# Softmax rows turned by VectorE in 32x32 blocks of 32-bit pairs instead of by TensorE, dense rows laid as 128 half rows, the maximum subtracted also on GpSimd

## The chip, the cores and the metric

One core of a Trainium2 chip. The metric is device microseconds (us) of one execution. The kernel before takes 1591.72 us (median of 3 runs, 1589.29 to 1592.78).

## The reference, cut to what matters

The input x has 2048 rows of 512 numbers. Two equal layers follow each other; each adds a recurrent attention and then a dense layer:

```python
x = x + A(layernorm(x)); x = x + B(layernorm(x))     # twice, with the same weights

def A(x):                        # 64 segments of 32 rows, in order
    mem = mem0                   # 8 rows
    for s in range(64):
        h = concat([mem, x[32*s : 32*s + 32]])        # L = 40 rows
        q, k, v = h @ Wq, h @ Wk, h @ Wv              # 32 heads of 128
        scores = where(mask, q @ k.T / sqrt(128), -1e9)     # 40 x 40 per head
        o = softmax(scores) @ v                       # per head
        o = o @ Wo                                    # summed over the heads, 40 x 512
        mem = o[:8]; out[s] = o[8:]
def B(x): return relu(x @ w1) @ w2                    # 512 -> 1376 -> 512
```

The memory of segment s is needed by segment s + 1, so the segments of one layer can't run side by side.

## The kernel before, in words

**Steps.** The kernel runs 66 steps. In step k it handles segment k of the first layer and segment k - 2 of the second (`DELTA = 2`), in the code the two values of `a`; in the first and last two steps only one is there. `HT` holds the 2 x 40 columns of both, transposed, so most matmuls have 80 columns.

**One step.** `queries_keys` makes q and k of eight or four heads at a time (TensorE, L726, from `HT`), evicted to `qT` and `kT` (`copy_op`, on ScalarE L982 or VectorE L984). The heads go in five units (`UNITS`): three of 8 heads and two of 4. For each unit `scores` does the softmax: score matmuls into PSUM (L1133), mask added (`block`, L1144), row maximum (`top`, L1148), subtraction (`sub`, L1151), exponential on ScalarE (`exp`, L1155), row sum (`total`, L1158), reciprocal (`recip`, L1161), scaling into `P` (`mul`, L1175, on VectorE or GpSimd). P has the queries of a head on the partitions, two heads of a pair at partitions 0 and 64. `turn` (L1181) multiplies each 128-column piece of P with an identity on TensorE, which turns it; `keep` copies the result twice from PSUM to `PT` (ScalarE L1198 or VectorE L1200), each time with one half of the partitions set to zero by `half`. `attend` multiplies the values (`V0` and `vw`) with PT (L1217), its result is evicted to `OT`, and `project` sums all heads into one PSUM bank (`st`). From that bank 16 columns go back into the next step's `HT` (the memories) and 64 into `OX`.

**The dense layer** of the step (`finish`) comes later, beside the next step's attention: `OX` is turned by a DMA into `y` (64 rows of 512), added to `x` (L924), normalized (`layernorm`: L749, L752, on GpSimd L731 and L736, then L755), turned by TensorE, multiplied with `w1` and `w2`; `total` (L940) adds the result in two halves of 256 columns, the second read from partition 64 of PSUM. The first layer's rows are normalized again and become columns of `HT` two steps later; the second layer's rows are narrowed on GpSimd and stored by one DMA.

**The order** is fixed before the kernel runs. `Plan.order` goes through all operations with an estimated cost for each (`t_dve(n)`, 0.07 us and 1.042 ns an element; `t_act`, `t_pool`) and writes them out; every engine then executes its own list strictly in that order and waits on semaphores. The tables `PLACE` (order of the TensorE operations by step and phase; phase 0 is a middle step), `PAIRED` (which matmuls run as two halves of 64 columns of weights) and `AHEAD` (priorities) steer it. An operation with two engines, such as `sub` after the change, gets its engine in that plan.

The score-side PSUM pool `b_work` has five banks; `scores` takes one for the scores (`sp`) and one for the turned rows (`tp`).

Of the kernel before, what the change touches and what calls it, by code (L numbers as in the profile page):

```python
# [9 lines left out]
F32 = mybir.dt.float32  # L10
# [20 lines left out]
LOOK = 0.0763052  # L31
PERIOD = 26.155362
PLACE = {
# [185 lines left out]


def t_dve(n, rate=1):
    return 0.07 + 1.042e-3 * n / rate


PART, MASKED = {ACT: 0.13, DVE: 0.10}, {ACT: 0.11, DVE: 0.065}
XBAR = 0.5, 0.2, 2.6


def t_pool(n):
    return 0.06 + 2.2e-3 * n  # L230

# [213 lines left out]
def kernel(  # L445
# [193 lines left out]
    def prepare():  # L639

        def zero_none():
            nc.vector.memset(none[:], 0.0)
# [733 lines left out]
```

## Time and profile before

| | us |
|---|---|
| median of 3 runs (lowest, highest) | 1591.72 (1589.29, 1592.78) |
| span of the profiled execution, first to last instruction | 1588.6 |
| TensorE matmul (PE), busy | 1569.5 |
| TensorE weight load (PEld), busy | 1411.1 |
| ScalarE (ACT), busy | 1165.2 |
| VectorE (DVE), busy | 1082.3 |
| GpSimd (POOL), busy | 314.3 |

The page gives the span as the only time of the profiled execution; it is 3.1 us under the median of the runs. A busy time is the union of an engine's instructions. Matmuls are pipelined: an 80-column matmul is recorded with some 200 ns, but 128 of them in a row take 4.61 us in the chain, 36 ns each. So a matmul's price is its distance to the next one, not its recorded duration, and the same holds in part for VectorE, where one instruction can start before the one ahead of it has ended.

### The profile page before, as it was taken

To read this page: it belongs to the slowest core of one execution; us is meant where nothing else is said; L and a number is where in the kernel's file an instruction comes from. 1 tells how busy PE (TensorE), PEld (TensorE's weight loads), DVE (VectorE), ACT (ScalarE), POOL (GpSimd) and SP (SyncE) were. 2 spreads that over 40 slices of the span, in tenths; PEclk is the share of its full clock that TensorE was granted. 3 is DMA by queue.
4 is the path that set the end of the run, shared out by engine and by line. 5 is a ranking of instruction groups with operands and counts; after the bars stand their busy time and mean duration, and the time that the engine had idled before them with its cause. 6 is when DMAs were issued, how large, how long until landed. Compare 5 with 4: busy or idle time off the path is not lost.

```text
span 1588.6 us, 100346 instructions
## 1 busy us (share of the span) xinstructions
PE 1569.5 (99%) x45458; PEld 1411.1 (89%) x45458; DVE 1082.3 (68%) x2957; ACT 1165.2 (73%) x3073; POOL 314.3 (20%) x667
## 2 busy tenths in 40 slices
PE   8999999999999999999999999999999999999998
PEld 5689999999999989999989999999998998898887
DVE  4566766766776776686676677677667667667665
ACT  4667777777777777777777777777777777777774
POOL 5112112212112212121121221211211121112110
PEclk9999999999999999999999999999999999999999
DMA  9711111111111111111111111111111111111100
GB/s 371 243 44 30 26 33 32 29 35 37 25 39 31 35 29 33 29 32 40 26 36 27 35 26 42 37 26 38 25 35 28 33 33 29 33 25 22 28 21 9
DMA packets 76540, 70.89 MB, mean 45 GB/s; under 512 B 50920, under 2 KB 62416, under 8 KB 76112
## 3 DMA queue, kind: packets, MB, share of 16 engines
q1 hardware_dynamic: 70096, 44.14, 13.1%
q0 software_dynamic: 4992, 19.40, 3.4%
q8 instruction: 356, 5.83, 1.6%
q10 hardware_dynamic: 1024, 0.93, 0.2%
q14 instruction: 72, 0.59, 0.1%
HBM read 31.53 MB, written 9.96 MB: 26 GB/s over the span
## 4 chain that ended last, share of the span: by engine, by line
PE 97%; DMA 1%; DVE 1%; POOL 1%; ACT 0%; issue 0%; DVEq 0%; POOLq 0%
PE work L726 40%; PE st L726 19%; PE fill L1048 16%; PE fill L726 8%; PE fill L821 5%; PE work L1217 5%; PE work L1133 4%; DMA xg<-in_A_x_dram 0%; DMA y<-OX 0%; DMA w_sb<-in_B_w_dram 0%; ACT HT L982 0%; POOL Wo_sb L537 0%; PE fill L711 0%; DVE ln L749 0%; POOL ln L736 0%
## 5 line engine op out<-in xcount | busy, mean ns | idle before, releaser
L726 PE MATMUL work<-HT,Wq_sb 128*128 128x80 bf16 (+2 forms) x10400 | 361.8, 201 | 3.1 <-ACT HT L982 3.1
L726 PE MATMUL work<-HT,Wk_sb 128*128 128x80 bf16 (+2 forms) x10416 | 362.7, 201 | 0.8 <-ACT HT L982 0.8
L726 PEld LDWEIGHTS <-Wq_sb 128*128 128x128 bf16 (+1 forms) x10400 | 330.9, 104 | 20.8 <-issue 6.0
L726 PE MATMUL st<-OT,Wo_sb 128*128 128x80 bf16 (+1 forms) x8448 | 345.5, 201 | 0.0
L726 PEld LDWEIGHTS <-Wk_sb 128*128 128x128 bf16 (+1 forms) x10416 | 327.1, 104 | 17.3 <-issue 2.0
L726 PEld LDWEIGHTS <-Wo_sb 128*128 128x128 bf16 x8448 | 315.7, 100 | 13.0 <-issue 12.7
L1048 PE MATMUL fill<-Wv_sb,HT 128*64 128x512 bf16 x2112 | 273.6, 381 | 1.1 <-DVE HT L984 1.0
L982 ACT CAST kT<-work 128x320 bf16<-128x320 f32 (+1 forms) x523 | 218.3, 418 | 68.6 <-PE work L726 31.1
L982 ACT CAST qT<-work 128x320 bf16<-128x320 f32 (+1 forms) x516 | 215.7, 418 | 67.5 <-PE work L726 47.2
L1198 ACT ACTIVATE PT<-work,half 128x160 bf16<-128x160 f32 (+1 forms) x515 | 231.3, 463 | 20.1 <-PE work L726 12.7
L982 ACT CAST OT<-work 128x320 bf16<-128x320 f32 (+1 forms) x461 | 186.2, 420 | 50.7 <-PE work L1217 50.6
L982 ACT CAST vw<-fill 128x512 bf16<-128x512 f32 x229 | 134.1, 586 | 113.3 <-PE fill L1048 109.8
L1144 DVE TENSOR_TENSOR es<-work,maskb 128x320 f32<-128x320 f32 (+2 forms) x330 | 136.2, 413 | 99.7 <-PE work L1133 93.2
L924 DVE TENSOR_TENSOR xg<-xg,y 64x512 f32<-64x512 f32 x65 | 44.2, 680 | 227.2 <-DMA y<-OX 226.6
L731 POOL TENSOR_SCALAR ln<-ln 32x1 f32<-32x1 f32 (+2 forms) x159 | 46.6, 293 | 566.7 <-DVE ln L752 561.0
L1155 ACT ACTIVATE es<-es 128x320 f32<-128x320 f32 (+2 forms) x330 | 136.1, 413 | 24.4 <-DVE es L1151 16.2
L1048 PEld LDWEIGHTS <-HT 128*64 128x64 bf16 x2112 | 98.9, 110 | 57.0 <-DVE HT L984 1.2
L1151 DVE TENSOR_TENSOR es<-es,mx 128x320 f32<-128x320 f32 (+2 forms) x330 | 136.3, 413 | 4.9
L1148 DVE TENSOR_REDUCE mx<-es 128x8 f32<-128x320 f32 (+2 forms) x330 | 133.9, 406 | 5.4
L1158 DVE TENSOR_REDUCE sm<-es 128x8 f32<-128x320 f32 (+2 forms) x330 | 133.4, 404 | 5.1 <-ACT es L1155 2.2
L1175 DVE TENSOR_TENSOR P<-es,sm 128x320 bf16<-128x320 f32 (+1 forms) x269 | 126.9, 472 | 3.3
L1133 PEld LDWEIGHTS <-qT 128*40 128x40 bf16 x4096 | 93.3, 97 | 35.6 <-ACT qT L982 13.6
(96 smaller groups left out, 2164.8 us busy)
## 6 DMA issues: line engine op xcount, KB each, us to landing
V<-vw SPq DMA_DIRECT2D x248, 48.0 KB
V<-vh SPq DMA_DIRECT2D x120, 64.0 KB
Wq_sb<-in_A_Wq_dram POOLq DMA_DIRECT2D x2, 2048.0 KB, 23.2
Wk_sb<-in_A_Wk_dram POOLq DMA_DIRECT2D x2, 2048.0 KB, 28.6
Wo_sb<-in_A_Wo_dram POOLq DMA_DIRECT2D x2, 2048.0 KB, 39.4
vh<-vg SPq DMA_DIRECT2D x32, 128.0 KB
xb<-in_A_x_dram SPq DMA_DIRECT2D x16, 128.0 KB
Wv_sb<-in_A_Wv_dram POOLq DMA_DIRECT2D x1, 2048.0 KB, 13.2
```

What stands on the lines that cost most here:

```text
L726: nc.tensor.matmul(out_[u:v, :], lhsT=lhsT[:, u:v], rhs=rhs, start=start, stop=stop, tile_position=(0, u), **more)
L821: nc.tensor.matmul(yp[64 * u:64 * u + 64, 0:256], lhsT=hT[:, fc, :], rhs=w2_sb[:, fc, 256 * u:256 * u + 256], start=(fc == 0), stop=(fc == ...
L982: nc.scalar.copy(out=out_, in_=in_)
L1048: nc.tensor.matmul(vp[64 * b:64 * b + 64, :], lhsT=cols(c4), rhs=Wv_sb[:, c4, n * 512:(n + 1) * 512], start=(c4 == 0), stop=(c4 == NC4 - 1 ...
L1133: nc.tensor.matmul(v[64 * g2:64 * g2 + L, a, i, b, :], lhsT=qT[:, hi, a * L:(a + 1) * L], rhs=kT[:, hi, a * L:(a + 1) * L], start=True, st ...
L1144: nc.vector.tensor_tensor(out=flat(es[:, A]), in0=flat(sp[:, A]), op=ALU.add, in1=maskb[:, a_lo:a_hi, :].unsqueeze(2).to_broadcast([128, n ...
L1148: nc.vector.tensor_reduce(out=mx[:, As], in_=es3(), axis=AX.X, op=ALU.max)
L1151: nc.vector.tensor_tensor(out=es3(), in0=es3(), op=ALU.subtract, in1=mx[:, As].unsqueeze(2).to_broadcast([128, ns * na, L]))
L1155: nc.scalar.activation(out=es[:, A], in_=es[:, A], func=ACTF.Exp, scale=SCALE)
L1158: nc.vector.tensor_reduce(out=sm[:, As], in_=es3(), axis=AX.X, op=ALU.add)
L1175: (nc.gpsimd if eng == POOL else nc.vector).tensor_tensor(out=o, in0=flat(es[:, A]), op=ALU.mult, in1=sm[:, As].rearrange("p (a s) -> p a ...
L1198: nc.scalar.activation(out=o, in_=i, func=ACTF.Copy, scale=half[:, b:b + 1])
```

## The change

- `turn` leaves TensorE. The two heads of a pair now lie next to each other as 16-bit numbers (index g, innermost), so that a pair of them is one 32-bit word, and VectorE's `transpose`, which turns each 32x32 block of 32-bit words by itself, turns two heads at once. Six instructions a unit: two over 64 partitions (64 words a row and pair of heads), which put all blocks, and four over 32 partitions, which write the blocks off the diagonal to their right place. Their inputs and outputs start at partitions 0, 32, 64 or 96. `PT` is zeroed once at the start, the masking copies (`keep`) and the bank `tp` are gone, and `attend` reads PT with a step of two elements.
- For that order the score tile is read from PSUM, the maximum and the sum from SBUF, with g innermost or with a step of two. `mul` of a unit of 8 heads becomes two instructions.
- `sub` may go to GpSimd or VectorE.
- The rows of the dense side are laid as 128 half rows (64 partitions for each 256 of the 512 columns, every other 128): `add`, the statistics, the normalization and `total` handle 256 elements on 128 partitions; the partial statistics are exchanged between the halves (`swap`, two small copies on ScalarE or VectorE). The turning matmuls are two instead of four. GpSimd's copies and the store are split into two.
- Memory is shared out anew (`y` and `ob` lie in `vx`, `none` in `P3`), and `PLACE`, `PAIRED`, `AHEAD` and `LOOK` are new numbers.

The core of the diff (the tables, the memory layout and the start are left out):

```diff
@@ layernorm of half rows, new
+    def layernorm_halves(x, keys, quick=False):
...
+            nc.vector.bn_stats(out=ln[:, 0:6], in_=x[:, :])
+        def swap(eng):
+            for u in range(2):
+                copy_on(eng, ln[64 * u:64 * u + 64, 8:14], ln[64 - 64 * u:128 - 64 * u, 0:6])
+        def aggr():
+            nc.vector.bn_aggr(out=ln[:, 6:8], in_=ln[:, :].rearrange("p (s f) -> p s f", s=2)[:, :, 0:6])
+        def norm():
+            nc.vector.tensor_scalar(out=xn[:, 0:256], in0=x[:, :], scalar1=ln[:, 6:7], scalar2=ln[:, 7:8],
+                                    op0=ALU.subtract, op1=ALU.mult)
@@ finish
         def add():
-            nc.vector.tensor_tensor(out=x[RB, :], in0=x[RB, :], in1=y[RB, :], op=ALU.add)
+            nc.vector.tensor_tensor(out=x[:, :], in0=x[:, :], in1=y[:, 0:256], op=ALU.add)
         def total(to):
-            for u in range(2):
-                cs = slice(256 * u, 256 * u + 256)
-                nc.vector.tensor_tensor(out=to[RB, cs], in0=x[RB, cs], in1=yp[64 * u:64 * u + 64, 0:256], op=ALU.add)
+            nc.vector.tensor_tensor(out=to[:, :], in0=x[:, :], in1=yp[:, 0:256], op=ALU.add)
@@ scores
         def block():
-            nc.vector.tensor_tensor(out=flat(es[:, A]), in0=flat(sp[:, A]), op=ALU.add,
-                                    in1=maskb[:, a_lo:a_hi, :].unsqueeze(2).to_broadcast([128, na, ns, L]))
+            nc.vector.tensor_tensor(out=ekg(), in0=sp[:, A].rearrange("p (j g k) -> p j k g", k=L, g=2), op=ALU.add,
+                                    in1=maskb[:, mine, :].unsqueeze(3).to_broadcast([128, nx * na, L, 2]))
...
-        plan.op(DVE, t_dve(n), sub, r=[mx], w=[es])
+        plan.op((POOL, DVE), (t_pool(n), t_dve(n)), sub, r=[mx], w=[es])
...
+        pieces = [(a, a + 1) for a in range(a_lo, a_hi)] if nx == 2 else [(a_lo, a_hi)]
         def mul(eng):
...
-        def turn(cols):
-            rhs = ident[:, :].rearrange("p (g q) -> p g q", g=2)[:, :, 0:L]
-            for a in range(a_lo, a_hi):
-                for i, x in enumerate(xs):
-                    z = nx * a + i
-                    c0 = 256 * a + 128 * x
-                    across(cols, tp[:, z * 2 * L:(z + 1) * 2 * L], P[:, c0:c0 + 128], rhs)
-        for b in range(2):
-            def keep(eng, b=b):
...
+        def turn():
+            i = P[:, 0:512].bitcast(F32).rearrange("p (j k) -> p j k", k=64)[:, mine, :]
+            o = PT[:, 0:nx * na, :, :].bitcast(F32)
+            for b in range(2):
+                R = slice(64 * b, 64 * b + 64)
+                nc.vector.transpose(out=o[R, :, b, :], in_=i[R, :, :])
+            for b in range(2):
+                R0, R1 = slice(64 * b, 64 * b + 32), slice(64 * b + 32, 64 * b + 64)
+                nc.vector.transpose(out=o[R0, :, b, 32:64], in_=i[R1, :, 0:32])
+                nc.vector.transpose(out=o[R1, :, b, 0:32], in_=i[R0, :, 32:64])
+        plan.op(DVE, 2 * t_dve(64 * na * nx) + 4 * t_dve(32 * na * nx), turn,
+                r=[*[("P", p, b, x) for b in range(2) for x in xs], "PT0"], w=[PT])
@@ attend
-                                             rhs=PT[:, a, 2 * i + h2, :, :], start=True, stop=True, tile_position=(0, u))
+                                             rhs=PT[:, (a - a_lo) * nx + i, :, :].rearrange("p b (q g) -> p b q g", g=2)[:, :, 0:L, h2],
+                                             start=True, stop=True, tile_position=(0, u))
@@ some of the new PLACE for a middle step, in their order
...
+    ("queries_keys.mmu1.2", 0): 65.109
...
+    ("scores.mmu1.0", 0): 66.065
+    ("scores.mmu0.0", 0): 67.104
+    ("scores.mmu2.0", 0): 67.827
+    ("scores.mmu3.0", 0): 72.231
+    ("scores.mmu4.0", 0): 77.413
+    ("attend.mmu1.0", 0): 81.682
+    ("attend.mmu0.0", 0): 81.683
+    ("attend.mmu2.0", 0): 84.931
+    ("attend.mmu3.0", 0): 87.378
+    ("attend.mmu4.0", 0): 87.783
+    ("project.mm.4", 0): 90.115
...
```

More of the change, by code (lines that the diff above doesn't have):

```diff
@@ new lines @@
+    ("*layernorm.aggr", 1): -21903.3, ("*make_mask", 1): -103617.438, ("*prepare_more.zero_ox", 1): 1.534,
+    ("*rstd.power", 1): 15.001, ("*rstd.raise_", 1): -61376.175, ("*turned.keep", 1): -24955.153,
+    ("*turned.turn", 1): 118381.72, ("*values.ev", 1): 0.807, ("*zero_columns.zero", 1): 0.064,
+    ("attend.ev", 0): -0.293, ("attend.ev", 1): 0.579, ("attend.ev", 2): -0.123, ("attend.mm", 1): 0.399,
+    ("attend.mm", 2): 1.152, ("bulk.land", 1): 26.171, ("clear_x.clear", 1): 20655.056,
@@ new lines @@
+    ("dense_layer.mm.da", 0): 0.236, ("dense_layer.mm.da", 2): 48.945, ("dense_layer.relu.da", 0): 100982.711,
+    ("dense_layer.relu.da", 1): 0.845, ("dense_layer.relu.da", 2): -11.721, ("finish.add", 1): -96751.759,
+    ("finish.narrow.db", 0): -0.422, ("finish.store.da", 2): -0.297, ("finish.store.db", 0): -10.15,
+    ("finish.total_out.da", 2): -52594.789, ("finish.total_x.da", 0): 2.7, ("finish.turn", 0): -40.658,
+    ("finish.turn", 1): -2.025, ("finish.turn", 2): 9.243, ("finish.turn_near", 2): -2.902,
@@ new lines @@
+    ("finish.widen", 0): -1.484, ("finish.widen", 1): 45455.413, ("get_x", 1): -82953.917, ("idle.spins", 2): -0.588,
+    ("late_values.mm", 0): 1.257, ("late_values.put", 0): 23.681, ("layernorm.aggr", 0): -28.708,
+    ("layernorm.aggr.dl", 0): 56094.205, ("layernorm.aggr.dl", 1): 83.393, ("layernorm.norm.dl", 1): 0.066,
+    ("layernorm.stats", 0): -254390.254, ("layernorm.stats.dl", 0): 2.212, ("layernorm.stats.dl", 1): 1.455,
+    ("layernorm_halves.aggr.da", 0): -7022.782, ("layernorm_halves.aggr.da", 2): -47028.151,
@@ new lines @@
+    ("prepare.place", 1): 9.977, ("prepare.turn", 1): 67303.233, ("prepare.zero", 1): 0.326,
+    ("prepare.zero_none", 1): 0.229, ("prepare_late.load", 0): -7.502, ("project.ev", 1): -6.419,
+    ("project.ev", 2): 64646.14, ("project.first", 1): -16.097, ("project.mm", 1): 2.102, ("project.mm", 2): 0.027,
+    ("project.rows", 0): -2.141, ("project.rows", 2): 0.044, ("queries_keys.ev", 0): 13.389,
+    ("queries_keys.ev", 1): -33.964, ("queries_keys.ev", 2): 0.003, ("queries_keys.mm", 0): -59260.586,
@@ new lines @@
+    ("scores.mul", 0): -0.605, ("scores.mul", 1): 47.888, ("scores.mul", 2): 58322.939,
+    ("scores.recip", 0): 96086.484, ("scores.recip", 1): -6.261, ("scores.recip", 2): 41.387,
+    ("scores.sub", 0): -142237.316, ("scores.sub", 1): -33204.156, ("scores.sub", 2): 1.026,
+    ("scores.top", 0): 154356.569, ("scores.top", 1): 8.385, ("scores.top", 2): 0.507,
+    ("scores.total", 0): -61524.001, ("scores.total", 1): 19.349, ("scores.total", 2): -4.942,
+    ("scores.turn", 1): 50960.199, ("scores.turn", 2): 19.857, ("turned.keep", 0): 0.081,
@@ L199 @@
+    ("turned.keep.da", 0): -14.11, ("turned.keep.da", 2): 53.845, ("turned.keep.db", 0): -0.106,
+    ("turned.keep.db", 1): -0.015, ("turned.turn", 0): -48305.91, ("turned.turn.da", 0): -2472.454,
+    ("turned.turn.da", 1): -6.507, ("turned.turn.da", 2): -71771.416, ("turned.turn.db", 0): -231.019,
+    ("turned.turn.db", 1): -6.756, ("values.ev", 0): -1.484, ("values.ev", 2): -20.456, ("values.mm", 0): 0.229,
+    ("values.mm", 1): -2.61,
 }
@@ L222, in t_dve @@
     return 0.07 + 1.042e-3 * n / rate
-PART, MASKED = {ACT: 0.13, DVE: 0.10}, {ACT: 0.11, DVE: 0.065}
+PART = {ACT: 0.13, DVE: 0.10}
 XBAR = 0.5, 0.2, 2.6
@@ L641, in zero_none @@
         def zero_none():
-            nc.vector.memset(none[:], 0.0)
+            nc.vector.memset(none[:, :], 0.0)
         def make_half():
@@ L671, in prepare @@
         plan.available("memory", 5.5)
-        plan.op(DVE, 0.17, zero_none, w=["none", "set"])
+        plan.op(DVE, 0.30, zero_none, w=["none", "set", *[("P", 3, b, x) for b in range(2) for x in range(2)]])
         plan.op(DVE, 0.4, make_half, w=["half", "set"])
@@ L676, in prepare @@
         parts = [([V0], 0.92, [("V0", q, b) for q in range(4) for b in range(2)] + [("V0l", b) for b in range(2)])]
-        parts += [([t], 0.30, [("P", p, b, x) for b in range(2) for x in range(2)]) for p, t in enumerate(Pt)]
+        parts += [([t], 0.30, [("P", p, b, x) for b in range(2) for x in range(2)]) for p, t in enumerate(Pt[:3])]
+        parts += [([t], 0.6, ["PT0"]) for t in p_PT.tiles]
         for tiles, t, w in parts:
@@ L710, in spin @@
         for u in range(2):
-            nc.tensor.matmul(bank[:, 256 * u:256 * u + 256], lhsT=none[:, 0:128], rhs=none[:, :], start=True, stop=True)
+            nc.tensor.matmul(bank[:, 256 * u:256 * u + 256], lhsT=none[:, 0:128], rhs=none[:, 0:256], start=True, stop=True)
     def idle(t, r=()):
@@ L762, in layernorm, with stats, turned @@
         return xn
-    def turned(xn, n, columns, copies):
+    def layernorm_halves(x, keys, quick=False):
+        ln, xn = p_ln.buf(), p_xr.buf()
+        R = slice(0, 128)
+        def stats():
+            nc.vector.bn_stats(out=ln[:, 0:6], in_=x[:, :])
[7 more added lines that the diff above has]
+                                    op0=ALU.subtract, op1=ALU.mult)
+        plan.op(DVE, t_dve(256), stats, r=keys, w=[ln])
+        plan.op((ACT, DVE), (0.2, 0.2), swap, w=[ln])
+        plan.op(DVE, 0.11, aggr, w=[ln])
+        rstd(ln, R, quick)
+        plan.op(DVE, 0.26, norm, r=[ln, *keys], w=[xn])
+        return xn
+    def turned(xn, n, columns, copies, blocks=NC4):
         tp = b_fill.buf()
+        wide = NC4 * n // blocks
         def turn(cols):
-            for c4 in range(NC4):
-                across(cols, tp[:, c4 * n:(c4 + 1) * n], xn[:, c4 * 128:(c4 + 1) * 128], columns)
-        plan.op(PE, 4 * t_mm(n), turn, r=[xn, "ident"], w=[tp], tile=EITHER, count=4, c64=4 * T64(n))
+            for c4 in range(blocks):
+                across(cols, tp[:, c4 * wide:(c4 + 1) * wide], xn[:, c4 * 128:(c4 + 1) * 128], columns)
+        plan.op(PE, blocks * t_mm(wide), turn, r=[xn, "ident"], w=[tp], tile=EITHER, count=blocks, c64=blocks * max(t_mm(wide), T64(n)))
         for size, out_, in_, r, w in copies:
@@ L787, in dense_layer @@
         n = 2 * SEG
-        xnT, xn = p_xm.buf(), layernorm(x, keys, slice(0, n), last)
-        turned(xn, n, ident[:, 0:n], [(NC4 * n, lambda: xnT[:, :, :], same, [], [xnT])])
+        xnT, xn = p_xm.buf(), layernorm_halves(x, keys, last)
+        turned(xn, n, ident[:, :], [(NC4 * n, lambda: xnT[:, :, :], same, [], [xnT])], 2)
         hT = p_h.buf()
@@ L887, in load_group @@
         plan.mark(plan.at[0], "")
-    Z = vx[:, 0:2, :].rearrange("p q n -> p (q n)").bitcast(F32)
-    R0, R1, RB = slice(0, SEG), slice(SEG, 2 * SEG), slice(0, 2 * SEG)
+    Z = vx[:, 0, :].bitcast(F32)
+    x_of = [t[:, 0:256] for t in xg]
     def clear_x():
@@ L902, in finish @@
         last = k == nsteps - 1
-        x, keys = xg[k % 2], [("x", k % 2, a) for a in range(2)]
+        x, keys = x_of[k % 2], [("x", k % 2, a) for a in range(2)]
         if 0 in act:
@@ L946, in total_out @@
             total(ob)
-        t_total = 2 * t_dve(256) + 2 * PART[DVE]
+        t_total = t_dve(256) + PART[DVE]
         if 0 in act:
@@ L1137, in flat @@
-        def flat(t):
-            return t.rearrange("p (a s k) -> p a s k", s=ns, k=L)
-        def es3():
-            return es[:, A].rearrange("p (s k) -> p s k", k=L)
+                for i in range(nx):
+                    for g in range(2):
+                        for b in range(2):
+                            (qT, kT), hi = (qk[b], 2 * i + g) if nx == 2 else (qk[0], 2 * b + g)
+                            nc.tensor.matmul(v[64 * b:64 * b + L, a, i, g, :], lhsT=qT[:, hi, a * L:(a + 1) * L],
+                                             rhs=kT[:, hi, a * L:(a + 1) * L], start=True, stop=True,
+                                             tile_position=(0, 64 * b))
@@ L1179, in scores @@
-        plan.op((POOL, DVE), (t_pool(n), t_dve(n)), mul, r=[es, sm], w=[("P", p, b, x) for b in range(2) for x in xs])
-        def turn(cols):
-            rhs = ident[:, :].rearrange("p (g q) -> p g q", g=2)[:, :, 0:L]
-            for a in range(a_lo, a_hi):
-                for i, x in enumerate(xs):
-                    z = nx * a + i
-                    c0 = 256 * a + 128 * x
-                    across(cols, tp[:, z * 2 * L:(z + 1) * 2 * L], P[:, c0:c0 + 128], rhs)
-        PT = p_PT.buf()
@@ L1190, in scores @@
-        plan.op(PE, nx * na * 0.0358, turn, r=[*[("P", p, b, x) for b in range(2) for x in xs], "ident"], w=[tp, PT],
-                tile=EITHER, count=nx * na)
-        for b in range(2):
-            def keep(eng, b=b):
-                o = PT[:, a_lo:a_hi, 0:2 * nx, b, :]
-                i = tp[:, A].rearrange("p (a g q) -> p a g q", g=2 * nx, q=L)
-                if eng == ACT:
-                    nc.scalar.activation(out=o, in_=i, func=ACTF.Copy, scale=half[:, b:b + 1])
-                else:
-                    nc.vector.tensor_scalar_mul(out=o, in0=i, scalar1=half[:, b:b + 1])
-            copy_op(n, keep, r=[tp, PT, "half"], w=[(PT, b)], more=MASKED)
+            for a0, a1 in pieces:
+                o = P[:, :].rearrange("p (a c) -> p a c", a=2)[:, a0:a1, 128 * xs[0]:128 * (xs[-1] + 1)]
+                o = (o[:, 0, :] if nx == 2 else o).rearrange("p x (k g) -> p x k g" if nx == 1 else "p (x k g) -> p x k g", k=64, g=2)
+                j = slice((a0 - a_lo) * nx, (a1 - a_lo) * nx)
+                (nc.gpsimd if eng == POOL else nc.vector).tensor_tensor(
+                    out=o[:, :, 0:L, :], in0=ekg()[:, j, :, :], op=ALU.mult,
+                    in1=by_head(sm)[:, j, :].unsqueeze(2).to_broadcast([128, nx * (a1 - a0), L, 2]))
@@ new lines, in scores @@
+        plan.op((POOL, DVE), (len(pieces) * t_pool(n / len(pieces)), len(pieces) * t_dve(n / len(pieces))), mul, r=[es, sm],
+                w=[("P", p, b, x) for b in range(2) for x in xs])
+        PT = p_PT.buf()
+        def turn():
[4 more added lines that the diff above has]
+                nc.vector.transpose(out=o[R, :, b, :], in_=i[R, :, :])
+            for b in range(2):
+                R0, R1 = slice(64 * b, 64 * b + 32), slice(64 * b + 32, 64 * b + 64)
+                nc.vector.transpose(out=o[R0, :, b, 32:64], in_=i[R1, :, 0:32])
+                nc.vector.transpose(out=o[R1, :, b, 0:32], in_=i[R0, :, 32:64])
```

176 lines of the change are left out of this document (74 added, 102 removed), and 224 rows, old and new, of tables (PAIRED, PLACE).

## The prediction

> **What bounds the kernel now.** I read the page's busy line first, then its chain, then one middle step in the windows view.
>
> ```profile
> PE 1569.5 (99%) x45458; PEld 1411.1 (89%) x45458; DVE 1082.3 (68%) x2957; ACT 1165.2 (73%) x3073; POOL 314.3 (20%) x667
> ...
> PE 97%; DMA 1%; DVE 1%; POOL 1%; ACT 0%; issue 0%; DVEq 0%; POOLq 0%
> ```
>
> TensorE has work nearly all the time and the chain runs along it. Busy here is not yet proof of a full engine, since a matmul recorded with 200 ns costs 36; but its waits are short too (the largest total, for HT, is 4.0 us in 14 waits). HT is written every 23.38 us in most steps (in the first steps and some others 23.8 or more), and 64 such periods make most of the 1588.6 us span. So a middle step is what counts. I cut one into three stretches: from its first q matmul to the first `block`, from there to the end of the last `mul`, and on to the next step's first q matmul.
>
> ```profile
> core 0: us, PE busy (x) PEld busy (x) DVE busy (x) ACT busy (x) POOL busy (x), PEclk, DMA share, GB/s
> 812.72:817.90 5.18, 5.18 (x150) 5.01 (x149) 1.48 (x3) 3.92 (x10) 0.79 (x2) 1.00 0.50 108
> 817.90:832.77 14.87, 14.87 (x461) 13.08 (x458) 14.13 (x41) 12.23 (x33) 2.82 (x7) 1.00 0.13 26
> 832.77:836.10 3.33, 3.33 (x91) 3.28 (x88) 1.12 (x3) 1.84 (x7) 1.29 (x3) 1.00 0.19 44
> ```
>
> The reader should see VectorE in the middle stretch: 14.13 of 14.87 us. Its 68% is an average over a stretch where it is nearly full and two where it has almost nothing to do, because the memories of the step are not there yet, or its softmax is done. TensorE is the bound today; VectorE is 0.7 us short of full in the stretch to which the change adds.
>
> **What leaves TensorE.** 16 turning matmuls in a middle step, at 36 ns (4.61 us for 128): 0.58 us. The turning of dense rows keeps its columns and loses two and two instructions, at most 0.04. So TensorE's floor goes from 23.38 to about 22.76 us a step. The stretched read of PT by `attend` has no row; I take it at nothing (no gain, since no column leaves it; at worst plus 32 x 36 ns = 1.15 us a step if it halved the rate). ScalarE loses most of `keep` (231.3 us in all) and can take evictions from VectorE; neither binds.
>
> **What goes on VectorE.** Durations by size come from the groups kept apart by shape:
>
> ```profile
> L1151 DVE TENSOR_TENSOR es<-es,mx 128x320 f32<-128x320 f32 x186 | 91.0, 489 | 2.6
> ...
> L1200 DVE TENSOR_SCALAR PT<-work,half 128x320 bf16<-128x320 f32 x121 | 65.9, 545 | 0.3
> ...
> L1151 DVE TENSOR_TENSOR es<-es,mx 128x160 f32<-128x160 f32 x136 | 43.5, 320 | 2.3
> ...
> L1175 DVE TENSOR_TENSOR P<-es,sm 128x160 bf16<-128x160 f32 x75 | 34.2, 455 | 0.2
> ```
>
> From 320 and 160 elements: 1.056 ns an element and 151 ns fixed, so 421 ns for 256 elements, 286 for 128, 219 for 64. A unit of 8 heads has two transposes of 256 words and four of 128 (1.99 us of durations), a unit of 4 heads two of 128 and four of 64 (1.45 us). What they cost depends on whether neighbours overlap, and the timeline shows both:
>
> ```profile
> 829.84 0.31 DVE L1158 TENSOR_REDUCE sm<-es 128x4 f32<-128x160 f32 x1
> 830.07 0.32 DVE L1151 TENSOR_TENSOR es<-es,mx 128x160 f32<-128x160 f32 x1
> 830.30 0.17 DVE L1161 RECIPROCAL sm<-sm 128x4 f32<-128x4 f32 x1
> 830.39 0.82 DVE L940 TENSOR_TENSOR vx<-xg,fill 64x256 f32<-64x256 f32 x2
> ```
>
> The reduction of 0.31 us is followed after 0.23: independent instructions overlap by 0.08. The two L940 need 0.82 us for two of 403 ns: they follow end to end, 0.01 us apart, although neither waits for the other. They differ from the rest in that the second reads from partition 64. Overlapping, a unit costs 1.99 - 6 x 0.083 = 1.49 us or 0.95; end to end 1.99 + 6 x 0.014 = 2.07 or 1.53. I take end to end, because the transposes are like L940 (their start partition changes each time) and the last four also overwrite what the first two wrote. A step then has 3 x 2.07 + 2 x 1.53 = 9.27 us of transposes, against 6.37.
>
> The Trainium skill ("VectorE: DVE Perf Modes", section "Two Vector instructions with no wait between them") says that an instruction starts only after all earlier ones have finished when its input or output starts in another group of 32 partitions than the last one in that memory. The trace shows that for PSUM only (L940); for SBUF, where the transposes work, no run here shows it yet. By the rule it is 9.27 us a step, without it 6.37.
>
> Now VectorE's need between the first `block` and the last transpose, instructions at duration less 0.083: for 8 heads `block`, `top`, `total` 0.41 each, `recip` 0.12, `mul` in two pieces 2 x 0.24, transposes 2.07: 3.88; for 4 heads 3 x 0.24 + 0.08 + 0.24 + 1.53 = 2.56. Together 16.8 us, with `sub` on GpSimd (the nearest GpSimd row, 160 elements of `mul`, has 454 ns; it overlaps VectorE's other units). The dense layer at half the elements: 0.34 + 0.34 + 0.09 + 0.27 = 1.04 before the first turn and as much for the second, 2.1 instead of some 3.9; loading x adds 0.26 a step; exchange and relu I put on ScalarE. Sum 19.1 us; up to 1.0 of it (the second dense part) may fall outside the stretch, and I count half: 18.6. Overlapping it would be 15.7.
>
> **Where it lands.** The step is a loop: memories, q and k, softmax, `attend`, `project`, memories. Ahead of the first `block` the new order has six groups of q and k matmuls instead of eight, so 5.18 - 2 x 0.575 = 4.03 us. Behind the last transpose stay `attend`, the eviction, the last `project` and the write to HT:
>
> ```profile
> 810.87 0.20 PE L1217 MATMUL work<-PT,V 128*128 128x80 bf16 x1
> ...
> 811.69 0.73 PE L726 MATMUL st<-OT,Wo_sb 128*128 128x80 bf16 x16
> ...
> 812.72 0.73 PE L726 MATMUL work<-HT,Wq_sb 128*128 128x80 bf16 x16
> ```
>
> That is 1.85 us, and 0.15 to hand over. The loop needs 4.03 + 18.6 + 2.0 = 24.6 us, over TensorE's 22.76 and over 23.38. `attend` of the last unit waits for `PT` from VectorE, and behind it in TensorE's fixed list wait `project` and the next step. So the saved 0.6 us turns into a wait of about 1.9. 62 middle steps x (24.6 - 23.38) = +76 us; the start's zeroing of PT (three memsets) lies under the loading of the weights (cover gone: under 3 us). 1588.6 + 76 = 1664.6, plus the 3.1 us by which the median of the runs lies over the span: 1668 us. Bounds of this case: with 1.0 us outside the stretch and smaller gaps 24.1 us, 1636; with the exchange on VectorE and the waits below 25.4 us, 1717.
>
> Edits without a price: turn DMA of `OX` at half the size (VectorE has been idle when it lands, 226.6 us of waits), two stores for one on SP (its queue waits 371.6 us for `ob` anyway; a second issue delays the loads behind it by one issue), GpSimd's copies in two pieces. If the store delayed `V` loads, `attend` would wait; I see no sign. `block` reading PSUM in alternating steps has no row: bounds 0 and a doubling of 3 x 0.34 + 2 x 0.17 us, 1.4 us a step; I take 0, the nearest row being the plain one.
>
> **Rivals.**
> 1. *TensorE stays the bound, faster.* If transposes overlap, the loop needs 4.03 + 15.7 + 2.0 = 21.7 us, less than 22.76, and the step follows TensorE: 62 x 0.62 = 38 us less, 1553 us. The turning point is 16.7 us of VectorE between `block` and last transpose. For it: all independent SBUF pairs overlap, and the planned cost in the diff is that of overlapping instructions. Against it: L940.
> 2. *GpSimd's subtraction holds up VectorE.* `mul` of 160 elements on VectorE has 455 ns on average where `sub` of the same size has 320; most of these `mul` run beside GpSimd's copy into `xg`, and so does the normalization of `vx` (664 ns, against 526 from `xg`, when GpSimd is idle). So VectorE instructions with two SBUF inputs are delayed by up to 0.17 us here, and more if GpSimd's instruction is longer. With 3.5 us of `sub` a step (two at the row's 0.45, three of twice the elements at an estimated 0.86) and eight `mul`, nearly always meeting one at 0.17: 1.3 us; on top of the forecast 62 x 1.3 = 81: 1749. The Trainium skill ("SBUF — State Buffer", section "SBUF: two separate sides") explains such rows by a shared port that one of the two holds for a whole instruction; by it the delay could reach the 0.86 us of a long `sub`.
> 3. *Nothing measurable*: the saving and the wait cancel, a step of 23.3 to 23.5 us. Needs luck.
>
> **How the numbers follow.** A measurement of this kernel can tell about 0.2% from no change, 3 us. Forecast 0.55 (1636 to 1717), rival 1 0.34 (about 1545 to 1585), rival 2 0.08, rival 3 0.03. Faster 0.34, same 0.03, slower 0.63. For 8 in 10 the range must hold both signs: 1547 to 1717.
>
> **What would show it.** Right: HT written every 24 to 25.5 us; TensorE idle before L1217 behind a transpose of `PT`, 1 to 2 us a step; transposes end to end at 0.42 and 0.29 us, some 570 us in all; VectorE over 80% busy. Wrong: a period under 23, transposes that start 0.08 us before the last one ends, PE without waits at `attend` (rival 1); `mul` far over 0.24 us beside a GpSimd `sub` (rival 2).

## The result, and the profile after

The changed kernel takes 1784.78 us (median of 4 runs, 1782.47 to 1787.59), the kernel before 1590.98 beside it: ratio 1.1219, 95% interval 1.1203 to 1.1235. The forecast was 1668 us, with a range up to 1717. The span grew by 195.9 us, from 1588.6 to 1784.5. In one of the runs below, two_starts, one execution of the four took 5305.61 us instead of some 1711; its ratio leaves that one out.

The busy line and the chain of the page after:

```profile
PE 1607.0 (90%) x44812; PEld 1399.1 (78%) x44812; DVE 1331.6 (75%) x4469; ACT 1070.5 (60%) x2915; POOL 486.2 (27%) x1147
...
DVE 59%; PE 30%; issue 6%; POOL 2%; DMA 2%; ACT 1%; SPq 0%; DVEq 0%; ACTq 0%; POOLq 0%
```

The chain has moved from TensorE (97% before) to VectorE (59%). TensorE's totals of waits (us in total, times, longest us) show where:

```profile
PE work L1246 <- DVE PT L1228: 119.1, 187, 1.4
```

L1246 is `attend` (L1217 before), L1228 the last transpose of a unit. The wait was 1 to 2 us a step, as forecast. The windows view of one middle step, cut like the one before the change (first q or k matmul to first `block`, to the end of the last transpose, to the next step's first matmul; the columns are the same):

```profile
888.77:892.80 4.03, 4.03 (x119) 3.93 (x118) 0.42 (x1) 2.99 (x8) 0.00 (x0) 1.00 0.13 29
892.80:912.99 20.19, 18.02 (x526) 15.44 (x524) 18.95 (x64) 12.25 (x34) 6.76 (x16) 1.00 0.07 15
912.99:914.89 1.90, 1.85 (x42) 1.68 (x41) 0.41 (x1) 0.95 (x4) 0.00 (x0) 1.00 0.15 47
```

The step is now this loop, 4.03 + 20.19 + 1.90 = 26.12 us. In the long stretch VectorE works 18.95 of 20.19 us; TensorE has 526 matmuls there and waits for it. One unit of 8 heads in the timeline of VectorE:

```profile
897.41 0.48 DVE L1180 TENSOR_REDUCE mx<-es 128x8 f32<-128x320 f32 x1
897.81 0.90 DVE L1224 STREAM_TRANSPOSE PT<-P 64x256 f32<-64x256 f32 x2
898.74 0.30 DVE L1227 STREAM_TRANSPOSE PT<-P 32x128 f32<-32x128 f32 x1
899.05 0.30 DVE L1228 STREAM_TRANSPOSE PT<-P 32x128 f32<-32x128 f32 x1
899.37 0.31 DVE L1227 STREAM_TRANSPOSE PT<-P 32x128 f32<-32x128 f32 x1
899.69 0.30 DVE L1228 STREAM_TRANSPOSE PT<-P 32x128 f32<-32x128 f32 x1
900.02 0.49 DVE L1176 TENSOR_TENSOR es<-work,maskb 128x320 f32<-128x320 f32 x1
```

The reduction is overtaken 0.08 us before its end, as most neighbours on VectorE are; from the first transpose on nothing overlaps. 897.81 to 900.02 is 2.21 us a unit (1.67 for 4 heads).

HT is written every 26.29 us on average over 58 middle steps, 23.49 before: 162 of the 196 us. Another 20 us are lost up to the fourth write of HT (at 150.9 us, before at 130.5), 13 in the last steps and behind them; what makes up these 13 is open. The start in the windows view, before and then after:

```profile
60.00:80.00 20.00, 17.47 (x410) 13.28 (x406) 13.63 (x48) 12.16 (x37) 4.93 (x11) 1.00 0.76 202
80.00:100.00 20.00, 19.75 (x555) 16.69 (x552) 12.42 (x35) 14.06 (x37) 1.82 (x5) 1.00 0.24 57
```

```profile
60.00:80.00 20.00, 16.08 (x371) 11.19 (x370) 12.50 (x51) 8.93 (x28) 2.40 (x6) 0.91 0.71 235
80.00:100.00 20.00, 14.80 (x349) 12.98 (x346) 8.88 (x34) 5.46 (x17) 4.12 (x11) 0.67 0.07 13
```

TensorE does 349 matmuls instead of 555 between 80 and 100 us, at a granted clock of 0.67.

### The profile page after: what moved, and what is told of

Read it like the earlier page. It is cut to its first block, busy times and chain, and to the rows that moved or that the text cites. A ratio compares the mean times of both kernels' runs of the same rounds, so it can differ in the third digit from the quotient of the medians.

```text
span 1784.5 us, 101088 instructions
## 1 busy us (share of the span) xinstructions
PE 1607.0 (90%) x44812; PEld 1399.1 (78%) x44812; DVE 1331.6 (75%) x4469; ACT 1070.5 (60%) x2915; POOL 486.2 (27%) x1147
## 4 chain that ended last, share of the span: by engine, by line
DVE 59%; PE 30%; issue 6%; POOL 2%; DMA 2%; ACT 1%; SPq 0%; DVEq 0%; ACTq 0%; POOLq 0%
PE work L723 18%; DVE PT L1224 12%; DVE PT L1228 9%; DVE PT L1227 9%; DVE es L1176 6%; DVE sm L1190 5%; DVE mx L1180 4%; PE st L723 4%; DVE P L1211 4%; PE fill L723 2%; PE fill L1076 2%; DVE sm L1193 2%; DVE xr L777 1%; DVE es L1183 1%; DVE vx L965 1%
## 5 line engine op out<-in xcount | busy, mean ns | idle before, releaser
L723 PE MATMUL work<-HT,Wq_sb 128*64 128x80 bf16 (+2 forms) x10432 | 373.4, 201 | 1.5 <-DVE es L1176 0.8
L1010 ACT CAST OT<-work 128x320 bf16<-128x320 f32 (+1 forms) x521 | 203.2, 418 | 175.4 <-PE work L1246 173.6
L1183 POOL TENSOR_TENSOR es<-es,mx 128x160 f32<-128x160 f32 (+2 forms) x209 | 116.0, 555 | 538.8 <-DVE sm L1193 351.4
L1224 DVE STREAM_TRANSPOSE PT<-P 64x256 f32<-64x256 f32 (+2 forms) x660 | 242.5, 367 | 10.8
L1010 ACT CAST qT<-work 128x320 bf16<-128x320 f32 (+1 forms) x470 | 196.8, 419 | 79.4 <-PE work L723 41.2
L1246 PE MATMUL work<-PT,V 128*64 128x80 bf16 (+1 forms) x1544 | 116.5, 200 | 117.1 <-DVE PT L1228 114.5
L1227 DVE STREAM_TRANSPOSE PT<-P 32x128 f32<-32x128 f32 (+2 forms) x660 | 180.1, 273 | 14.8
L728 POOL TENSOR_SCALAR ln<-ln 128x1 f32<-128x1 f32 x159 | 42.1, 265 | 532.5 <-DVE ln L774 401.9
L1228 DVE STREAM_TRANSPOSE PT<-P 32x128 f32<-32x128 f32 (+2 forms) x660 | 180.1, 273 | 9.0
L1246 PEld LDWEIGHTS <-vw 128*64 128x64 bf16 (+1 forms) x1530 | 85.5, 104 | 124.9 <-issue 116.8
L950 DVE TENSOR_TENSOR xg<-xg,vx 128x256 f32<-128x256 f32 x65 | 27.1, 418 | 187.8 <-DMA vx<-OX 187.6
```

What stands on the lines that cost most here:

```text
L723: nc.tensor.matmul(out_[u:v, :], lhsT=lhsT[:, u:v], rhs=rhs, start=start, stop=stop, tile_position=(0, u), **more)
L1010: nc.scalar.copy(out=out_, in_=in_)
L1183: (nc.gpsimd if eng == POOL else nc.vector).tensor_tensor(out=ekg(), in0=ekg(), op=ALU.subtract, in1=by_head(mx).unsqueeze(2).to_broadcast ...
L1224: nc.vector.transpose(out=o[R, :, b, :], in_=i[R, :, :])
L1227: nc.vector.transpose(out=o[R0, :, b, 32:64], in_=i[R1, :, 0:32])
L1228: nc.vector.transpose(out=o[R1, :, b, 0:32], in_=i[R0, :, 32:64])
```

## The experiments

Theory A is the forecast's: the transposes, held back by their changing start partitions, make VectorE's stretch the longest part of a loop that TensorE must wait for. The rivals put the loss into the order, into GpSimd's subtraction, or into the length of the softmax as such.

**Same start partition.** All six transposes read and write from partition 0; number, sizes and order stay.

```diff
-                R = slice(64 * b, 64 * b + 64)
+                R = slice(0, 64)
...
-                R0, R1 = slice(64 * b, 64 * b + 32), slice(64 * b + 32, 64 * b + 64)
+                R0 = R1 = slice(0, 32)
```

> The changed kernel with the six transposes of a unit all starting at partition 0, in the same number, sizes and order, each still overwriting part of what an earlier one wrote (the rows turned are the wrong ones, so the output is not the reference's). In the changed kernel's trace each transpose starts 0.014 to 0.031 us after the last one ended, even where it has no wait. Theory A (the start partition makes VectorE finish everything first, and VectorE's work between first mask and last transpose sets the step): they overlap by 0.08, a unit's six become 0.63 us shorter, five units 3.2 us a step, 62 steps: about 1590 us. Where the overwriting ones wait for the first two, only four of the six gaps close: 0.42 us a unit, 1655. Rival (the transpose as such is never overlapped, wherever it starts): gaps as before, 1785.

Measured 1589.45 us, ratio to before 0.9992 (0.9983 to 1.0001). All 195 us are gone. The chain is `PE 91%`, HT comes every 23.07 us in most steps. VectorE's timeline for one unit of 8 heads:

```profile
825.74 0.75 DVE L1224 STREAM_TRANSPOSE PT<-P 64x256 f32<-64x256 f32 x2
826.42 0.26 DVE L1227 STREAM_TRANSPOSE PT<-P 32x128 f32<-32x128 f32 x1
826.62 0.26 DVE L1228 STREAM_TRANSPOSE PT<-P 32x128 f32<-32x128 f32 x1
826.81 0.26 DVE L1227 STREAM_TRANSPOSE PT<-P 32x128 f32<-32x128 f32 x1
827.00 0.26 DVE L1228 STREAM_TRANSPOSE PT<-P 32x128 f32<-32x128 f32 x1
827.20 0.44 DVE L1176 TENSOR_TENSOR es<-work,maskb 128x320 f32<-128x320 f32 x1
```

The same six instructions take 1.46 instead of 2.21 us: each starts 0.06 to 0.07 us before its predecessor ends, and the recorded durations are shorter too (0.26 instead of 0.30). That the expected 1590 us came out is partly luck: 0.75 us a unit was freed and not 0.63, so 3.75 us a step, but TensorE's own 23.07 us let only 3.0 of it through (26.29 to 23.30 on average).

**Without the small transposes.** A unit has two transposes left.

```diff
-            for b in range(2):
-                R0, R1 = slice(64 * b, 64 * b + 32), slice(64 * b + 32, 64 * b + 64)
-                nc.vector.transpose(out=o[R0, :, b, 32:64], in_=i[R1, :, 0:32])
-                nc.vector.transpose(out=o[R1, :, b, 0:32], in_=i[R0, :, 32:64])
```

> The changed kernel without the four transposes over 32 partitions (the blocks off the diagonal are left wrong); same planned order on every engine. They take 1.27 us in a unit of 8 heads and 1.0 in one of 4 in the changed kernel's trace, 5.8 us a step. Theory A (VectorE's stretch sets the step): head 4.0, stretch 20.2 - 5.8, tail 1.9 give 20.3 us, less than TensorE's own 22.8 to 23, so TensorE is the bound again: HT every 23 us, 1570 to 1590 us with what the start loses. Rival C (the new order of TensorE, its switches and the start cost the time): over 1700.

Measured 1587.37 us, 0.9979 (0.9969 to 0.9988). TensorE is the bound again (HT every 23.07 us in most steps, as in same_start); taking still more from VectorE brings hardly anything.

**Which changes of start hold.** The six transposes of a unit at other places, so that some neighbours share both starts, some differ in the output's alone and some in the input's alone.

```diff
+                R0, R1 = slice(64 * b, 64 * b + 32), slice(64 * b + 32, 64 * b + 64)
                 nc.vector.transpose(out=o[R, :, b, :], in_=i[R, :, :])
...
+                for u in range(2):
+                    if b == 0:
+                        nc.vector.transpose(out=o[R1, :, b, 32 * u:32 * u + 32], in_=i[R0, :, 32:64])
+                    else:
+                        nc.vector.transpose(out=o[R0, :, b, 32 * u:32 * u + 32], in_=i[R1, :, 0:32])
```

> The kernel after with the six transposes of a unit at other places (the blocks off the diagonal are not all put where they belong): 64 partitions from 0 to 0, then twice 32 partitions from 0 to 32, then 64 from 64 to 64, then twice 32 from 96 to 64. Theory A (an instruction is held until the earlier ones have finished when its input or output starts at another partition than that of the one before): the second of each equal pair overlaps its predecessor by 0.06 us as in same_start, the others follow at +0.01 to +0.03; an output change alone (0 to 32) and an input change alone (64 to 96) hold both. Four changes a unit instead of six; same_start saved 0.74 us a unit for six, 0.123 each, so 5 x 2 x 0.123 = 1.23 us a step less, HT every 25.0 us, 1785 - 62 x 1.23 = 1709 us. Rival 1: an instruction whose input and output start at different partitions is itself slow, changed or not: no pair overlaps, 1785 us. Rival 2: only changes of the output hold: the pair 64 to 64, 96 to 64 overlaps too, three changes, about 1670 us.

Measured 1711.29 us, 1.0761 (1.0743 to 1.0779); HT every 25.2 us on average. VectorE's timeline for a unit of 8 heads:

```profile
840.80 0.38 DVE L1225 STREAM_TRANSPOSE PT<-P 64x256 f32<-64x256 f32 x1
841.22 0.49 DVE L1228 STREAM_TRANSPOSE PT<-P 32x128 f32<-32x128 f32 x2
841.73 0.44 DVE L1225 STREAM_TRANSPOSE PT<-P 64x256 f32<-64x256 f32 x1
842.21 0.50 DVE L1230 STREAM_TRANSPOSE PT<-P 32x128 f32<-32x128 f32 x2
842.74 0.32 DVE L1176 TENSOR_TENSOR es<-work,maskb 128x160 f32<-128x160 f32 x1
```

The two L1228 have different starts for input and output, but the same as each other: together they take 0.49 us at 280 ns each on average, so they overlap. The first of them (output moved from 0 to 32) and the first L1230 (input moved from 64 to 96) both wait for the end of the one before. So it is the change that holds, of the input or of the output; rivals 1 and 2 of this run are out. The price of 0.123 us for a change, taken from same_start, gave 1709.

This is the rule of the Trainium skill ("VectorE: DVE Perf Modes", section "Two Vector instructions with no wait between them"), which the prediction could check for PSUM only; the trace agrees for SBUF, with gaps of +0.01 to +0.03 us where a start changes and -0.06 to -0.08 where none does.

**The order.** The kernel after, planned anew:

```diff
-        plan.op(DVE, 2 * t_dve(64 * na * nx) + 4 * t_dve(32 * na * nx), turn,
+        plan.op(DVE, 2 * t_dve(64 * na * nx) + 4 * t_dve(32 * na * nx) + 0.70, turn,
```

> The kernel after, with 0.70 us more in the cost that the planner is told for the six transposes of a unit (2.19 instead of 1.49 us for 8 heads), so that order and choice of engines are made anew with about what they take. Theory A: the stretch is the sum of VectorE's work and no order shortens it; 1770 to 1800 us. Rival: the loss comes from an order made for cheaper transposes (qT evictions and sub on VectorE at the wrong time), and with the true cost most of 2 us a step comes back: under 1700.

Measured 1801.95 us, 1.1339 (1.132 to 1.1358). That is 2 us over Theory A's range and 17 us slower than the kernel after: told the true cost, the planner finds no better order with the same tables, so the rival is out. That no order at all would be better is not shown.

**Subtraction on GpSimd alone, on VectorE alone.** `sub` is forced on one engine, at its place in the order of after (first GpSimd; for the second run the same line has `nc.vector`).

```diff
-            (nc.gpsimd if eng == POOL else nc.vector).tensor_tensor(out=ekg(), in0=ekg(), op=ALU.subtract,
+            nc.gpsimd.tensor_tensor(out=ekg(), in0=ekg(), op=ALU.subtract,
```

> The changed kernel with every subtraction of the maximum on GpSimd, nothing else moved in any engine's order. VectorE loses two of 0.4 us in a step's stretch; GpSimd's takes 0.72 us and two handovers more, and VectorE's next sum waits for it. Theory A: the two nearly cancel, 0 to -0.8 us a step, 1735 to 1785 us. Rival B (GpSimd's instructions hold up VectorE's): longer scaling instructions beside them, more than 1800.

Measured 1818.91 us, 1.1435 (1.1418 to 1.1452), so B's side of that forecast. The group of `mul`, first of after, then of this kernel (count, busy us, mean ns):

```profile
L1211 DVE TENSOR_TENSOR P<-es,sm 128x160 bf16<-128x160 f32 x310 | 89.9, 322 | 2.0
```

```profile
L1211 DVE TENSOR_TENSOR P<-es,sm 128x160 bf16<-128x160 f32 x310 | 122.8, 428 | 4.1
```

VectorE's `mul` takes 316 ns where GpSimd is idle (130 cases) and 584 where it runs beside GpSimd's subtraction of 320 elements (122 cases, medians); `block` and the reductions, with one input from SBUF, show no such difference where they meet one (before_sub, below: `block` of 160 elements 325 ns beside it, 324 alone). Five `mul` a step at 0.106 us more are 0.53. The two `sub` that VectorE no longer does would have given 0.84 back, but in the step looked at (908.39 to 929.07, 20.68 us) `total` of the first unit comes no earlier, since it now waits for the longer GpSimd instruction (3.22 us behind the first `block`, 3.15 in after). Of the 0.40 of the other one, 0.29 goes into waits, 0.10 us ahead of `mul` and 0.19 ahead of the next `total`, which again needs GpSimd's result through the exponential. The period is 26.80, 0.51 us more than in after. The mechanism of the prediction's rival 2 exists, but it has no part in the kernel after: none of its 318 `mul` on VectorE runs beside a subtraction on GpSimd.

> The changed kernel with every subtraction on VectorE, nothing else moved. Three more a step in the stretch, 0.4 + 2 x 0.24 = 0.9 us. Theory A: up to +0.9 us a step, less where VectorE waited for GpSimd: 1800 to 1840. Rival B (GpSimd was holding VectorE up): 1785 or less.

Measured 1897.89 us, 1.1928 (1.191 to 1.1947), more than either theory said. The head and the tail of most steps stay at 4.03 and 1.9 us; it is the stretch that grows, from 20.2 to 21.8 us (medians). In one step (stretch 804.48 to 826.08, 21.60 us) three more `sub` are 0.89 us of work; the rest is mostly new waiting: each stands behind the transposes of another unit, and `total` then waits for the exponential, three times 0.2 to 0.3 us. TensorE also waits for ScalarE's eviction of q (51.9 us in 58 waits, in after not among the listed rows). In this step that wait is inside the stretch, and its reason is the same late `sub`: ScalarE's list stands 2.09 us at the exponential that needs it, with the eviction behind. VectorE's list goes on meanwhile.

**The parts alone.** First the half rows alone: `finish`, `layernorm_halves`, `turned` and the memory layout of after, with `scores`, `attend` and the tables of before.

> The dense side of the change alone: rows laid as 128 half rows, softmax and its turning on TensorE as before, with the order tables of before (so the start is not tuned to it). Theory: the half rows cost TensorE more columns, which my prediction took at nothing. In the trace of same_start the turning and memory matmuls of a step (34 of 128x64, 24 of 64-row 64, 4 of 64-row 128) take 1.134 + 0.380 + 0.215 = 1.73 us, in the kernel before (48 of 128x64, 4 of 128x32) 1.399 + 0.106 = 1.505. So HT every 23.38 + 0.22 = 23.60 us in most steps, and 1591 + 62 x 0.22 = 1604 us, up to 1616 if the start loses the 11 us that it loses in same_start. Rival (the prediction's term): no column more and two instructions less, 23.34 us a step, 1588 us plus what the start loses.

Measured 1610.55 us, 1.0132 (1.0117 to 1.0147). HT every 23.51 us in most steps against 23.38: +0.13, not the 0.22 expected, and not the gain that the prediction had put there. The reason expected is wrong too. By the distances of matmuls in the two traces, the dense turning and the matmuls with w1 (named "turning and memory matmuls" above) take 1.50 us in such a step and 1.51 in the kernel before, so the half rows give TensorE no more work. The 0.13 us is a wait: the last turning matmul of the softmax starts 0.159 us behind the one before it, where 0.036 is usual, and 0.058 us after the end of `mul` on VectorE. Directly ahead of that `mul`, VectorE's list now has the exchange of the statistics (two copies, 0.50 us). 13 of the 21 us are lost before the fourth write of HT (143.7 us, before 130.5), where TensorE waits once for 10.8 us for a normalized x (L779); the tables were not made for this kernel. Then the softmax side alone: `scores`, `attend` and the tables of after, with the dense functions of before on rows of 512.

> The softmax side of the change alone: pairs turned by VectorE, sub and mul on GpSimd or VectorE, with the order tables of after; the dense rows stay 64 rows of 512 (y and ob lie in vx, since the memory would not suffice). Theory A (the step is the loop memories, q and k, VectorE's softmax, attend, project): the dense layer on 512 columns puts 1.2 to 1.8 us a step back on VectorE's stretch, HT every 27.3 to 27.9 us (26.1 to 26.3 in after), 1785 + 62 x 1.2 to 1.8 = 1859 to 1897 us. Rival: the dense layer lies beside VectorE's waits (for the statistics' exchange, for x), and the half rows save nothing on the path: 1775 to 1800.

Measured 1910.22 us, 1.2016 (1.1999 to 1.2034), 13 us over the expected range; HT every 27.5 us in its most common steps, 28.25 on average. TensorE's wait for transposes has nearly doubled:

```profile
PE work L1217 <- DVE PT L1199: 222.3, 188, 2.5
```

So the half rows cost 21 us where TensorE is the bound, in waits and not in matmuls, and save 125 where VectorE is: 1910 to 1785 (the planner's choices of engine shift with them).

This kernel also shows where same_start's 1.73 us of those matmuls come from. With full rows of 512 and the tables of after they take 1.75 us. The new order runs one group of 12 matmuls with w1, and one dense turning, as halves of 64 columns of weights. The halves with w1 in turn_only, then in half_only, which has the tables of before:

```profile
L725 PE MATMUL fill<-xnM,w_sb 128*64 128x64 bf16 x1576 | 36.0, 196 | 0.6 <-ACT xnM L981 0.5
L725 PE MATMUL fill<-xnM,w_sb 128*64 128x64 bf16 x168 | 3.5, 196 | 0.5 <-ACT xnM L1012 0.5
```

Then GpSimd's subtraction alone, in the kernel before:

```diff
-            nc.vector.tensor_tensor(out=es3(), in0=es3(), op=ALU.subtract,
+            nc.gpsimd.tensor_tensor(out=es3(), in0=es3(), op=ALU.subtract,
...
-        plan.op(DVE, t_dve(n), sub, r=[mx], w=[es])
+        plan.op(POOL, t_pool(n), sub, r=[mx], w=[es])
```

> The kernel before with one part of the change alone: the maximum is subtracted on GpSimd, in all units (order planned anew with the old tables). VectorE loses 186 x 0.41 + 136 x 0.24 = 109 us of work, 1.7 us a step; the subtraction takes 0.72 and 0.45 us on GpSimd instead of 0.49 and 0.32, and VectorE's mul takes 0.58 instead of 0.32 us for 160 elements when it meets one (sub_gpsimd). Theory A: TensorE stays the bound, VectorE has 1.7 us more room than it needs for the delays; HT every 23.4 us, 1585 to 1597 us. Rival B: the longer chain of a unit (0.23 us each, and the delayed mul) ends last in the middle stretch, where VectorE had 0.7 us of room; HT every 24.0 us or more, over 1620 us.

Measured 1626.81 us, 1.0231 (1.0215 to 1.0246). Theory A of this run was wrong, and the time is on rival B's side: 1.7 us a step less on VectorE made the step longer, 23.93 us in most. TensorE's waits have one new row, and the timeline shows its place (the turning matmul of a unit waits for `mul`):

```profile
PE work L726 <- DVE P L1175: 22.9, 61, 0.7
```

```profile
825.36 1.32 PE L726 MATMUL st<-OT,Wo_sb 128*128 128x80 bf16 x32
827.04 0.25 PE L726 MATMUL work<-ident,P 128*128 128x80 bf16 x2 [0.36 <-DVE P L1175]
```

From the start of the last L726 before it to this matmul it is 0.56 us, where 0.04 is usual: nearly all of the 0.55 us by which the step is longer (the wait is shown with 0.36, since the matmul before is recorded with 0.2). What ends last here is not VectorE's sum of work but a chain of instructions, in which GpSimd's subtraction takes longer than VectorE's (0.72 us for 0.49) and the dense layer's normalization beside it 0.77 us for 0.53; which of the two decides was not separated.

**The start.** The load of the second group of x is put ahead of the loads of w1 on SP's list.

```diff
-        for o in plan.order():
+        ops = plan.order()
+        o = next(o for o in ops if o.kind == "load_group.load.dl")
+        ops.remove(o)
+        ops.insert(next(i for i, d in enumerate(ops) if d.kind == "load_dense.dma1"), o)
+        for o in ops:
```

> The kernel after with one DMA moved: the load of the second group of x (xb) is issued on SP ahead of the loads of w1, instead of behind them. In after SP stands at the first w1 load (L552) from about 52 us until a store has freed the place (54.8 to 58.5 us), the load of x follows at 59.4 and lands at 67.4; VectorE's list waits for it, and the turn DMA of OX queues behind its successor. Theory: this is most of the start's loss (second period 38.5 us against 25.3 before, 3.4 us of it VectorE's wait for xb, some 7 us the late turn DMA); 4 to 8 us come back, 1777 to 1781 us, HT in the middle steps unchanged at 26.1 to 26.3. Rival: the second period is the order of TensorE's list, and nothing changes: 1785 us.

Measured 1782.59 us, 1.1208 (1.1191 to 1.1225): against after that can't be told from no change. In the trace the fourth write of HT comes 3.0 us earlier (147.8), less than expected.

The same with all transposes at partition 0:

> same_start (all six transposes read and write from partition 0, so the blocks are not put where they belong) with the load of x moved as in early_xb. TensorE is the bound there, HT every 23.07 us in most steps, mean 23.30. Theory: what the start gives back shows in full, 1589.5 - 4 to 8 = 1581 to 1585 us. That is the best the change's structure could give if the holds cost nothing; rival 1 of the prediction priced it at 1553. Rival: the start's loss is the order's, 1589 us.

Measured 1583.32 us, 0.9955 (0.9938 to 0.9972); same_start had 0.9992 (0.9983 to 1.0001), so here some 6 us show. The fourth write of HT is at 138.2 us, 3.2 earlier than in same_start and still 7.7 later than before. The load's place on SP explains a small part of the start's loss; what makes up the rest was not separated.

Of the kernels that do all of the work, none is faster than the kernel before.

## Why the prediction was wrong in size and right in kind

- **Mechanism, right.** VectorE's stretch became the bound, `attend` waits for the last transposes, the transposes go end to end. The other branch is real too: with 0.75 us a unit less (same_start) the step follows TensorE. Head and tail were as worked out: 4.03 us for 4.03, 1.90 for 2.0.
- **The stretch, mis-sized: 20.19 us for 18.6.** This is the term that failed; 26.29 - 24.6 = 1.7 us a step on average, 62 x 1.7 = 105 of the 120 us by which the span (1784.5) exceeds the forecast's (1664.6). By its pieces, in the step shown: `sub` was put on GpSimd altogether, but VectorE does two a step, 0.84 us; an eviction of q stands in VectorE's list, 0.50; it waits 0.28 us for the exchange of the statistics and 0.27 for q; the transposes take 3 x 2.2 + 2 x 1.67 = 9.9 instead of 9.27. Against that, three `mul` instructions a step are on GpSimd, and the dense layer in the stretch has 1.58 us instead of 1.86. The bound of 25.4 us a step had allowed only for the exchange on VectorE and waits. Nor would `sub` on GpSimd altogether have brought the sum down to 18.6: where it is so (sub_gpsimd) the stretch shown is 20.68 us, with waits for GpSimd's instruction and a `mul` lengthened by it, both of which the sum had at nothing.
- **VectorE "over 80% busy", wrong**: 75%. The step grew with the work.
- **TensorE's floor, wrong, hidden by the result: 23.07 us (same_start) for 22.76.** The softmax's 16 turning matmuls did go (0.59 us by the distances of matmuls in the two traces, 0.58 forecast). The dense turning, taken at "at most 0.04" less, is right as long as the matmuls stay whole: with those of w1 1.50 us instead of 1.51 (half_only). But the new order runs some of them as halves, 1.73 us (same_start; 1.75 in turn_only without half rows): the order's own cost to TensorE had no term. The stretched read of PT, taken at nothing, cost 0.04. So with these tables rival 1's 1553 us was out of reach: with the holds gone the kernels take 1583 to 1589 us, about the kernel before. As it was ordered, the change could not have gained what it was credited with even on its best branch.
- **The start, mis-sized: "under 3 us" for 20.** Only the zeroing of PT was priced there; the new order of the first steps was not. The 11 us of it that same_start shows, where no transpose is held, cancel what the steps gain there (58 x 0.20 us).
- **Rival 2**: priced at 0.17 us for each meeting, 0.27 measured, but only in sub_gpsimd, with all `sub` on GpSimd; in after there is no such meeting.

## What to carry to other kernels

When several short instructions with different start partitions replace one operation, price them end to end and count the changes of start of inputs and outputs; grouping equal starts together wins the overlap back. When an operation may go to either of two engines, price both choices: the cheaper one for an engine's sum may lengthen the chain or meet another instruction at a shared input. And before crediting a saving, work out the floor of the next bound from the instructions that the new order really issues, split ones included, not from the elements alone.

## What the runs showed of the hardware

- For VectorE's transposes a start partition in SBUF that changes between 0, 32, 64 and 96, of the input or of the output, costs about 0.12 us: the lost overlap, and a longer recorded instruction (a 32x128 transpose of 32-bit words is recorded with 257 ns in same_start and 303 in after).
- VectorE's instruction with two SBUF inputs beside GpSimd's takes 584 ns instead of 316. The Trainium skill ("SBUF — State Buffer", section "SBUF: two separate sides") calls it a shared pair of ports that one of the two holds for its whole instruction; the longest `mul`, 847 ns, is 531 more than 316, less than the 0.78 us that GpSimd's instruction takes on average, which fits. In before_sub the normalization of 64x512, beside GpSimd's subtraction, takes 770 ns instead of 534.
- Where TensorE had gaps in the start, its granted clock was 0.67 on average from 80 to 100 us, and 0.50 from 80 to 90; the 44 matmuls with w1 at 88.2 us took 2.51 us, where a middle step of the kernel before needs 1.28 for as many. The kernel before, with more work in the same 20 us, kept 1.00. That the gaps brought the clock down is not shown.
